# Linear attention and a multiplicative feed-forward on one core: batch 0's third and fourth query chunks, the order of two weight loads, and the last batch's layout

## The chip, the cores and the metric

The kernel runs on 1 core of one Trainium2 chip. The metric is the device time in microseconds of one execution; a kernel's time is the median of its runs. The profiled execution is one run with the hardware profiler on; its span is the time from its first to its last instruction in the profile.

## The reference

Eight batches, eight heads, 576 positions, 64 dimensions. The features of q and k are `relu(x)` times a cosine and a sine of the position, side by side, so 128 features per head. The attention is linear (no softmax). Its output, laid out as 4608 tokens by 512, goes through a feed-forward that is linear behind a product of two projections:

```python
kv  = einsum('bhsf,bhsd->bhfd', phi(k), v)
z   = phi(k).sum(axis=2)
num = einsum('bhsf,bhfd->bhsd', phi(q), kv)
den = einsum('bhsf,bhf->bhs', phi(q), z)[..., None] + 1e-06
x   = (num / den).transpose(0, 2, 1, 3).reshape(4608, 512)
out = ((x @ w1) * (x @ w2)) @ w3 @ w_out      # 512->1024, 1024->1024, 1024->512
```

## The kernel before

**Attention, by batch.** A batch's 576 positions are five chunks: four of 128 rows and one of 64 (the "half chunk", chunk 4). `features` makes cosine features on VectorE (L270) and sine features on ScalarE (L274), in bf16. `kv_first` (batch 0) and `kv_chunk` (L305) multiply k's features with v and a column of ones, so that the denominators come along. For a query chunk, the features must be transposed (features on the partitions): by TensorE into a bank of the accumulator memory and an eviction (`q_tr`, L336), or by a DMA transpose issued on SP's queue (`transpose_q`, L283). `num` (L365) multiplies them with the kv state, and VectorE normalizes (L381 to L383: denominator, reciprocal, product) into a block `xblk`. `x_tr` transposes that block again, by TensorE and an eviction (L417, L419) or by a DMA, into `xT`, the feed-forward's input.

**Feed-forward, by tiles.** Nine tiles of 512 tokens. `ffn_groups(t)` is a generator that makes one group of products per step: `products` (L462, w1 and w2), ScalarE copies one side out, VectorE multiplies with the other (L468, L519) into `abT`, and products with `w34b` (L532) give the output, which ScalarE evicts (L539) into `osb`. `w34b = w3 @ w_out` is computed once, in tile 0: for each of eight 128-row blocks of w3, `w3_tr` (L225) transposes the block on TensorE and VectorE copies it, and `w34_mm` (L237) multiplies it with w_out, in two parts of four products (part 0 reads w_out's first half, part 1 its second).

**The order is written by hand.** Between feed-forward groups, numbered slots run the functions entered by `at(slot, ...)`. Every engine executes its own instructions in that program order and waits on semaphores for data and for buffers. Tile 0's first four column blocks are made in two halves of 256 tokens, the first as quarters of 128, so that the first group can start when the first chunk (128 tokens) of `xT` is there, and the second quarter when the second chunk is there (slot 1 makes it).

**The start.** Lines 589 to 620 run ahead of slot 0. `idle_mms` are products of zeros whose result is not read. For chunk 0 the transposes are evicted by VectorE in halves; chunks 1, 2 and 3 are evicted by ScalarE (`q_tr(..., evac=False)[1]()`). The transposes of `q_tr`, `x_tr` and `w3_tr` share two buffers of one bank each (`ps_tr`). Chunk 3's transposes stand in slot 1, its cosines and sines at L606 and L607. The idle products' bank, `unread`, and the bank beside it belong to the pool `ps_idle`, which is closed when the feed-forward's four banks are opened.

**Queues.** All casting loads are issued on GpSimd's queue, in program order: v, q in two halves of columns, w1 and w2 in blocks of 256 columns, the half chunk of q (L201), then a block of w1. `other_loads` (L204) waits by a small copy for the first `xblk`, and issues the rest of w1 and w2, then `w3` block 0, w_out half 0, `w3` block 1, w_out half 1, `w3` blocks 2, 3, 4 and 5, batch 1's k, and `w3` blocks 6 and 7. An issue also waits until the load eight places before it has landed. SP's queue holds k's loads of batch 0, the DMA transposes and, at the end, the stores of the last tile; other stores are GpSimd's.

**Layouts.** Batches 1 to 6 are loaded in two parts: positions 0 to 319 into partitions 0 to 63 (five per partition), and 320 to 575 into partitions 64 to 127 (four per partition). Batch 0, and before the change also batch 7, are loaded as rows 0 to 511 over 128 partitions (four per partition) and rows 512 to 575 (the half chunk). `rows_of` gives the matching pieces of the output: one piece of 128 rows for batches 0 and 7, two of 64 for the others. The last tile of all (t = 8) holds chunks 0 to 3 of batch 7; its last 128 tokens are made, evicted (L550) and stored in two halves of 256 columns.

Of the kernel before, what the change touches and what calls it, by code (L numbers as in the profile page):

```python
# [68 lines left out]
def kernel(  # L69
# [41 lines left out]
    def load(b, which, part=None):  # L111
        for name in which:
            src = {"k": k, "v": v, "q": q}[name]
            if b == B - 1:
                if part == 0:
                    raw[b, name] = ld.tile([P, H, NCH, D], BF16, name=name + "s",
                                           bufs=2 if name == "q" else 1)
                (load_first4 if part else load_first)(nc.gpsimd, raw[b, name], src, b=b)
                continue
            if part != 1:  # L120
                raw[b, name] = ld.tile([P, H, NCH, D], BF16, name=name + "s",
                                       bufs=2 if name == "q" else 1)
                nc.gpsimd.dma_start(
                    out=raw[b, name][0:64, :, :, :].rearrange("p h j d -> p h (j d)"),
                    in_=src[b, :, 0:320, :].rearrange("h (p j) d -> p h (j d)", j=5))
            if part != 0:
                nc.gpsimd.dma_start(
                    out=raw[b, name][64:128, :, 0:4, :].rearrange("p h j d -> p h (j d)"),
                    in_=src[b, :, 320:S, :].rearrange("h (p j) d -> p h (j d)", j=4))

    def load_first(eng, t, src, c0=0, n=4, b=0):
        rows = src[b, :, 0:512, :].rearrange("h (p j) d -> p h j d", j=4)
        eng.dma_start(out=t[:, :, c0:c0 + n, :].rearrange("p h j d -> p h (j d)"),  # L133
                      in_=rows[:, :, c0:c0 + n, :].rearrange("p h j d -> p h (j d)"))

    def load_first4(eng, t, src, b=0):
        eng.dma_start(out=t[0:64, :, 4, :], in_=src[b, :, 512:S, :].rearrange("h p d -> p h d"))

    woutb = wst.tile([P, 8, DM], BF16, name="woutb")
    w3b = wst.tile([P, 8, DFF], BF16, name="w3b")  # L140
# [6 lines left out]
    def load_w3(jp, n):  # L147
        nc.gpsimd.dma_start(out=w3b[:, jp:jp + n, :],
                            in_=moe_w3[ds(jp * P, n * P), :].rearrange("(b p) l -> p b l", p=P))

    def load_wout(half):
        nc.gpsimd.dma_start(out=woutb[:, ts(half, 4), :],
                            in_=moe_w_out[ts(half, 512), :].rearrange("(c p) m -> p c m", p=P))
# [29 lines left out]
    def idle_mms(n):  # L183

        for _ in range(n):
            nc.tensor.matmul(unread[:, :], lhsT=zeros[:, 0:128], rhs=zeros[:], start=True, stop=True)
# [11 lines left out]

    load_w12(0, 256)
    load_w12(256, 256)  # L200
    load_first4(nc.gpsimd, q0, q)  # L201
    nc.gpsimd.dma_start(out=w1b[:, :, ds(512, 256)], in_=w1v[:, :, ds(512, 256)])

    def other_loads(behind):  # L204

        seen = sm.tile([P, 1], BF16, name="seen", bufs=1)
        nc.gpsimd.tensor_copy(out=seen[:], in_=behind)
        nc.gpsimd.dma_start(out=w2b[:, :, ds(512, 256)], in_=w2v[:, :, ds(512, 256)])
        load_w12(768, 256)
        for jp in range(2):  # L210
            load_w3(jp, 1)
            load_wout(jp)
        for jp in range(2, 4):
            load_w3(jp, 1)
        load_w3(4, 2)
        load(1, "k")
        load_w3(6, 2)
# [47 lines left out]
    def features(b, dst, src, c, cos=True, sin=True, scalar_heads=H):  # L265

        R = ROWS[c]
        at = c if b in (0, B - 1) else NCH + c
        if cos:
            nc.vector.tensor_scalar(out=dst[:R, c, :, 0:D], in0=src[:R, :, c, :], scalar1=0.0,  # L270
                                    scalar2=cosv[:R, at:at + 1], op0=ALU.max, op1=ALU.mult)
        if sin:
            n = scalar_heads
            nc.scalar.activation(out=dst[:R, c, 0:n, D:F], in_=src[:R, 0:n, c, :], func=ACTF.Relu,  # L274
                                 scale=sinv[:R, at:at + 1], bias=0.0)
            if n < H:
                nc.vector.tensor_scalar(out=dst[:R, c, n:H, D:F], in0=src[:R, n:H, c, :],
                                        scalar1=0.0, scalar2=sinv[:R, at:at + 1],
                                        op0=ALU.max, op1=ALU.mult)
# [51 lines left out]
    def q_tr(b, c, evac=True):  # L331
        R = ROWS[c]
        qp = feat[b][1]
        pst = ps_tr.tile([P, 8, 128], BF16, name="pst")
        for h in range(H):
            nc.tensor.transpose(pst[:, h, :], qp[:, c, h, :], identb[:])  # L336
        dst, src = att_of(b)["qpT"][:, :, ds(columns_of(b, c), R)], pst[:, :, 0:R]
        on_vector = lambda: nc.vector.tensor_copy(out=dst, in_=src)
        on_scalar = lambda: nc.scalar.copy(out=dst, in_=src)
        if evac:  # L340
            on_vector()
        return on_vector, on_scalar
# [55 lines left out]

    xT = {}

    def x_tr(b, c, by_vector=False):
        R, rows = ROWS[c], out_rows(b, c)
        xblk = att[b]["x"].pop(c)
        xf = xblk[:].rearrange("p g h d -> p (g h d)")
        if b % 2 == 0:
            slot = S * b + 128 * c
        else:
            slot = S * b + (0 if c == 4 else 64 + 128 * c)
        t, o = divmod(slot, 512)
        if t not in xT:  # L410
            xT[t] = xtp.tile([P, 4, 512], BF16, name="xT")
        if b >= 2 or (b, c) in ((0, 4), (1, 3)):
            nc.sync.dma_start_transpose(out=xT[t][:, :, ds(o, R)], in_=xf[rows])
            return
        pst = ps_tr.tile([P, 8, 128], BF16, name="pst")
        for kc in range(4):
            nc.tensor.transpose(pst[:, kc, :], xf[:, ts(kc, 128)], identb[:])  # L417
        copy = nc.vector.tensor_copy if by_vector else nc.scalar.copy
        copy(out=xT[t][:, :, ds(o, R)], in_=pst[:, 0:4, rows])  # L419

    def rows_of(b, c, n):

        if b in (0, B - 1):
            rows = out[ds(b * S, S), :]
            if c == 4:
                return [rows[512:S, :].rearrange("(p j) m -> p j m", j=1)]
            return [rows[0:512, :].rearrange("(p j) m -> p j m", j=4)[:, c:c + n, :]]
        lower = out[ds(b * S, 320), :].rearrange("(p j) m -> p j m", j=5)
        upper = out[ds(b * S + 320, 256), :].rearrange("(p j) m -> p j m", j=4)
        return [h[:, c:c + n, :] for h in ((lower,) if c == 4 else (lower, upper))]  # L430

    def store(eng, osb, g, n, cols=slice(0, DM)):

        pair, r = divmod(g, 9)
        b, c = (2 * pair, r) if r < 4 else (2 * pair + 1, r - 5)
        if r == 4:
            parts = rows_of(2 * pair, 4, 1) + rows_of(2 * pair + 1, 4, 1)
        elif n == 1 or c + n <= 4:
            parts = rows_of(b, c, n)
        else:  # L440
            parts = None
        if parts is None or (r == 4 and n > 1):
            for i in range(n):
                store(eng, osb[:, i:i + 1, :], g + i, 1, cols)
            return
        for i, rows in enumerate(parts):
            eng.dma_start(out=rows[:, :, cols], in_=osb[64 * i:64 * i + rows.shape[0], :, cols])  # L447

    ffn_tiles = [0]

# [5 lines left out]
    def ffn_groups(t):  # L456
# [86 lines left out]
        if t == NT - 1:  # L543
            for half in range(2):
                cols = ts(half, 256)
                ops = ffn_tile()
                for jc in range(8):
                    nc.tensor.matmul(ops[:, 0:256], lhsT=abT[:, jc, ts(3, 128)],  # L548
                                     rhs=w34b[:, jc, cols], start=(jc == 0), stop=(jc == 7))
                nc.scalar.copy(out=osb[:, 1, cols], in_=ops[:, 0:256])  # L550
                store(nc.sync, osb[:, 1:2, :], 4 * t + 3, 1, cols)
                yield


# [47 lines left out]
    idle_mms(1)  # L602
    num(0, 0)
    q_tr(0, 1, evac=False)[1]()
    other_loads(att[0]["x"][0][:, 0, 0, 0:1])
    features(0, q0f, q0, 3, sin=False)  # L606
    features(0, q0f, q0, 3, cos=False)  # L607
    idle_mms(2)
    x_tr(0, 0, by_vector=True)
    num(0, 1)  # L610
    q_tr(0, 2, evac=False)[1]()
    ps_ffn = []
    for stack in first:
        stack.close()
# [2 lines left out]
                                                     space=bass.MemoryType.PSUM)))  # L617


    at(1, lambda: x_tr(0, 1, by_vector=True), lambda: q_tr(0, 3, evac=False)[1](), lambda: num(0, 2))  # L620
    at(3, lambda: x_tr(0, 2), lambda: num(0, 3))
    at(5, lambda: x_tr(0, 3))
    at(6, lambda: features(0, q0f, q0, 4))
    at(23, lambda: transpose_q(0, 4))
    at(7, lambda: load(1, "qv"), lambda: load(2, "q"))
    at(29, lambda: num(0, 4))
# [70 lines left out]
```

## Time and profile before

| what | value |
|---|---|
| time, median of 3 runs | 248.81 us (248.33 to 248.97) |
| profiled execution, own time | 248.81 us |
| its span | 246.9 us |
| TensorE products (PE), busy | 240.5 us, 97% |
| VectorE (DVE), busy | 135.9 us, 55% |
| ScalarE (ACT), busy | 130.2 us, 53% |
| GpSimd (POOL), busy | 93.4 us, 38% |
| granted TensorE clock | 1.0 |

How to read it: an engine that is busy 97% of the span sets the time, so what counts is where it is idle or does work that nobody needs, and which event ends each of these stretches. Engines at about half of the span matter only where TensorE waits for them. In the timelines a row gives start and duration in microseconds, the engine, the source line, the operation, what it writes and reads, its shape and count; a bracket gives the idle time before it and what ended it. The landing time of a load is its issue time plus its time to landing.

The longest waits of TensorE in the whole execution:

```profile
PE unread L186 <- DVE zeros L162: 1.2, 1, 1.2
PE kva L322 <- DVE va L297: 1.2, 1, 1.2
PE pst L349 <- DVE qp L277: 0.3, 1, 0.3
```

(waiting line, what it waited for, total us, times, longest.) The first two lie ahead of batch 0's kv products, at the very start.

### The profile page before, as it was taken

The page shows a single profiled execution, that of the slowest core. Times are in us where ns is not written, and L with a number is a line of the kernel's source. Part 1 is how long each engine was busy: PE and PEld are TensorE (multiplying, and loading weights), DVE is VectorE, ACT ScalarE, POOL GpSimd, SP SyncE. Part 2 cuts the span into 40 slices and gives each one's busy share as a digit, 9 for nine tenths or more (in the row PEclk, how much of TensorE's full clock was granted, in tenths as well). Part 3 has the DMA queues.
Part 4 walks back from the last instruction along what each step waited for, and adds up shares of the span by engine and source line. Part 5 has one row for each costly group of instructions (what it writes and reads, how often), then busy time and mean ns, then how long its engine had stood idle before and what let it go on. Part 6 is the DMA issues. An engine that isn't in the chain of part 4 may idle for free.

```text
span 246.9 us, 5034 instructions
## 1 busy us (share of the span) xinstructions
PE 240.5 (97%) x1872; PEld 130.4 (53%) x1872; DVE 135.9 (55%) x336; ACT 130.2 (53%) x266; POOL 93.4 (38%) x196
## 2 busy tenths in 40 slices
PE   8799999999999999999999999999999999999994
PEld 3479545566975445444544555454545554444443
DVE  7775652668968445647566475547464645312420
ACT  2676313767943873466556654854575333434332
POOL 7654342024512261127032612173322005978700
PEclk9999999999999999999999999999999999999999
DMA  7999999999999969999999999999994536998823
GB/s 199 178 194 199 201 207 204 198 181 173 153 162 142 167 100 149 132 149 134 169 144 155 118 180 150 150 140 140 166 142 89 94 64 214 260 281 289 282 101 128
DMA packets 86200, 41.22 MB, mean 167 GB/s; under 512 B 53792, under 2 KB 82720, under 8 KB 86176
## 3 DMA queue, kind: packets, MB, share of 16 engines
q0 software_dynamic: 37008, 27.20, 71.8%
q1 hardware_dynamic: 49168, 13.71, 35.9%
q8 instruction: 14, 0.23, 0.4%
q14 instruction: 10, 0.08, 0.1%
HBM read 38.80 MB, written 9.44 MB: 195 GB/s over the span
## 4 chain that ended last, share of the span: by engine, by line
PE 85%; DMA 10%; POOL 3%; issue 1%; ACT 0%; POOLq 0%
PE ffnps L462 45%; PE ffnps L532 24%; PE ffnps L237 6%; DMA woutb<-in_moe_w_out_dram 5%; DMA w2b<-in_moe_w_dram 5%; PE pnum L365 4%; PE pnum L305 4%; PE pst L225 1%; PE ffnps L548 1%; POOL qs L133 1%; POOL w1b L196 1%; PE pst L336 1%; POOL vs L133 0%; PE pst L417 0%; POOL w2b L197 0%
## 5 line engine op out<-in xcount | busy, mean ns | idle before, releaser
L462 PE MATMUL ffnps<-xT,w2b 128*128 128x512 bf16 (+2 forms) x344 | 75.5, 344 | 0.0
L462 PE MATMUL ffnps<-xT,w1b 128*128 128x512 bf16 (+2 forms) x344 | 75.5, 344 | 0.0
L519 DVE TENSOR_TENSOR abT<-asb,ffnps 128x512 bf16<-128x512 bf16 x64 | 43.9, 686 | 54.3 <-PE ffnps L462 52.4
L532 PE MATMUL ffnps<-w34b,abT 128*128 128x512 bf16 x280 | 65.0, 379 | 0.0
L515 ACT CAST asb<-ffnps 128x512 bf16<-128x512 f32 x64 | 37.4, 584 | 50.0 <-PE ffnps L462 45.2
L462 PEld LDWEIGHTS <-w2b 128*128 128x128 bf16 x344 | 31.0, 98 | 27.3
L462 PEld LDWEIGHTS <-w1b 128*128 128x128 bf16 x344 | 30.8, 98 | 25.9
L567 POOL COPY seen<-mark 1x1 bf16<-1x1 bf16 x50 | 8.9, 178 | 84.4 <-ACT mark L565 84.4
L532 PEld LDWEIGHTS <-abT 128*128 128x128 bf16 x280 | 26.0, 98 | 27.9 <-DVE abT L519 0.2
L539 ACT COPY osb<-ffnps 128x512 f32<-128x512 f32 x35 | 20.5, 584 | 35.2 <-PE ffnps L532 35.1
L274 ACT ACTIVATE qp<-qs,sinv 128x512 bf16<-128x512 bf16 (+2 forms) x40 | 28.1, 714 | 1.8 <-DMA qs<-in_q_dram 1.8
L383 DVE TENSOR_TENSOR xblk<-pnum,den 128x512 bf16<-128x512 f32 (+1 forms) x37 | 25.6, 691 | 1.3
L297 POOL COPY va<-vs 128x512 bf16<-128x512 bf16 (+1 forms) x30 | 17.6, 621 | 22.9 <-DMA vs<-in_v_dram 22.4
L274 ACT ACTIVATE kp<-ks,sinv 128x512 bf16<-128x512 bf16 (+1 forms) x35 | 25.0, 717 | 0.9 <-DMA ks<-in_k_dram 0.9
L447 POOL DMA_DIRECT2D out_dram<-osb x42 | 22.1, 531 | 2.7 <-issue 2.1
L365 PEld LDWEIGHTS <-qpT 128*128 128x128 bf16 x320 | 15.4, 98 | 8.7 <-DVE qpT L350 0.6
L381 DVE TENSOR_SCALAR den<-pnum 128x8 f32<-128x8 f32 (+1 forms) x37 | 6.0, 163 | 22.6 <-PE pnum L365 22.5
L237 PE MATMUL ffnps<-woutb,w3T 128*128 128x512 bf16 x64 | 15.8, 380 | 0.2 <-DMA woutb<-in_moe_w_out_dram 0.2
L365 PE MATMUL pnum<-kvs,qpT 128*128 128x65 bf16 x296 | 15.8, 194 | 0.0
L270 DVE TENSOR_SCALAR qp<-qs,cosv 128x512 bf16<-128x512 bf16 (+1 forms) x40 | 15.3, 389 | 0.7 <-DMA qs<-in_q_dram 0.7
L305 PEld LDWEIGHTS <-kp 128*128 128x128 bf16 x280 | 11.4, 98 | 4.1
L270 DVE TENSOR_SCALAR kp<-ks,cosv 128x512 bf16<-128x512 bf16 (+1 forms) x35 | 12.5, 367 | 0.0
(88 smaller groups left out, 181.6 us busy)
## 6 DMA issues: line engine op xcount, KB each, us to landing
out_dram<-osb POOLq DMA_DIRECT2D x16, 256.0 KB, 4.5
out_dram<-osb POOLq DMA_DIRECT2D x24, 128.0 KB, 3.9
qs<-in_q_dram POOLq DMA_DIRECT2D x8, 256.0 KB, 7.6
ks<-in_k_dram POOLq DMA_DIRECT2D x6, 320.0 KB, 6.3
qs<-in_q_dram POOLq DMA_DIRECT2D x6, 320.0 KB, 5.9
vs<-in_v_dram POOLq DMA_DIRECT2D x6, 320.0 KB, 5.7
ks<-in_k_dram POOLq DMA_DIRECT2D x6, 256.0 KB, 7.0
vs<-in_v_dram POOLq DMA_DIRECT2D x6, 256.0 KB, 5.4
```

The source lines that it names most:

```text
L237: nc.tensor.matmul(acc[:, :], lhsT=w3T[:, lc, :], rhs=woutb[:, lc, :], start=(lc == 0), stop=(lc == 7))
L270: nc.vector.tensor_scalar(out=dst[:R, c, :, 0:D], in0=src[:R, :, c, :], scalar1=0.0, scalar2=cosv[:R, at:at + 1], op0=ALU.max, op1=ALU.mult)
L274: nc.scalar.activation(out=dst[:R, c, 0:n, D:F], in_=src[:R, 0:n, c, :], func=ACTF.Relu, scale=sinv[:R, at:at + 1], bias=0.0)
L305: nc.tensor.matmul(kvt[:, h // 4, ds((h % 4) * 65, 65)], lhsT=kp[:, c, h, :], rhs=va[:, c, h, 0:D + 1], start=(i == 0 and h % 4 == 0), sto ...
L365: nc.tensor.matmul(banks[h // 4][:, ds((h % 4) * 65, 65)], lhsT=qpT[:, h, ds(at, 128)], rhs=kvs[:, h, :], start=True, stop=True)
L383: nc.vector.tensor_tensor(out=xblk[rows, g], in0=n4[:, :, :, 0:D], in1=den[rows, g].unsqueeze(3).to_broadcast([R, G, 4, D]), op=ALU.mult)
L447: eng.dma_start(out=rows[:, :, cols], in_=osb[64 * i:64 * i + rows.shape[0], :, cols])
L462: nc.tensor.matmul(out, lhsT=w[:, kc, ts(jc, 128)], rhs=x[:, kc, tok], start=(kc == 0), stop=(kc == 3))
L515: nc.scalar.copy(out=asb[:], in_=aT[:, :])
L519: nc.vector.tensor_mul(out=abT[:, jc, :], in0=asb[:], in1=bT[:, :])
L532: nc.tensor.matmul(ops[:, :], lhsT=abT[:, jc, ts(ms, 128)], rhs=w34b[:, jc, :], start=(jc == 0), stop=(jc == 7))
L539: nc.scalar.copy(out=osb[:, ms % 2, :], in_=ops[:, :])
```

## The change

Four things are changed.

- **The order at the start.** Chunk 2's transposes are issued ahead of the transposes of the first `xblk`, and two idle products there are dropped. The first block is transposed into a new tile of the idle products' bank and evicted by ScalarE instead of VectorE; chunk 2's eviction follows it on ScalarE. Chunk 3's transposes move from slot 1 to the place where chunk 2's stood.
- **The sines of chunk 3** are made by one GpSimd instruction instead of one of ScalarE. It stands on GpSimd's queue ahead of `other_loads`.
- **Loads.** The half chunk of q is loaded behind `w3` block 1 instead of ahead of the third w1 block, and its features move from slot 6 to slot 19. Both halves of w_out are loaded ahead of `w3` block 1.
- **The last batch** is loaded and stored in the layout of batches 1 to 6. So each store of 128 rows in the last tile becomes two of 64; the two of the very last stores' pieces are issued on SP and on ScalarE.

```diff
@@ load
-            if b == B - 1:
-                if part == 0:
-                    raw[b, name] = ld.tile([P, H, NCH, D], BF16, name=name + "s",
-                                           bufs=2 if name == "q" else 1)
-                (load_first4 if part else load_first)(nc.gpsimd, raw[b, name], src, b=b)
-                continue
@@ loads of the start
     load_w12(256, 256)
-    load_first4(nc.gpsimd, q0, q)
     nc.gpsimd.dma_start(out=w1b[:, :, ds(512, 256)], in_=w1v[:, :, ds(512, 256)])
@@ other_loads
-        for jp in range(2):
-            load_w3(jp, 1)
-            load_wout(jp)
+        load_w3(0, 1)
+        for half in range(2):
+            load_wout(half)
+        load_w3(1, 1)
+        load_first4(nc.gpsimd, q0, q)
@@ features
-        at = c if b in (0, B - 1) else NCH + c
+        at = c if b == 0 else NCH + c
@@ x_tr
-        pst = ps_tr.tile([P, 8, 128], BF16, name="pst")
+        if pst is None:
+            pst = ps_tr.tile([P, 8, 128], BF16, name="pst")
@@ rows_of
-        if b in (0, B - 1):
+        if b == 0:
@@ store
-            eng.dma_start(out=rows[:, :, cols], in_=osb[64 * i:64 * i + rows.shape[0], :, cols])
+            on = eng[i % 2] if isinstance(eng, tuple) else eng
+            on.dma_start(out=rows[:, :, cols], in_=osb[64 * i:64 * i + rows.shape[0], :, cols])
@@ ffn_groups, last tokens
-                store(nc.sync, osb[:, 1:2, :], 4 * t + 3, 1, cols)
+                store((nc.sync, nc.scalar), osb[:, 1:2, :], 4 * t + 3, 1, cols)
@@ the start
     q_tr(0, 1, evac=False)[1]()
+    nc.gpsimd.tensor_scalar(out=q0f[:, 3, :, D:F], in0=q0[:, :, 3, :], scalar1=0.0,
+                            scalar2=sinv[:, 3:4], op0=ALU.max, op1=ALU.mult)
     other_loads(att[0]["x"][0][:, 0, 0, 0:1])
     features(0, q0f, q0, 3, sin=False)
-    features(0, q0f, q0, 3, cos=False)
-    idle_mms(2)
-    x_tr(0, 0, by_vector=True)
+    by_scalar = q_tr(0, 2, evac=False)[1]
+    x_tr(0, 0, pst=ps_idle.tile([P, 8, 128], BF16, name="unread"))
+    by_scalar()
     num(0, 1)
-    q_tr(0, 2, evac=False)[1]()
+    q_tr(0, 3, evac=False)[1]()
@@ slots
-    at(1, lambda: x_tr(0, 1, by_vector=True), lambda: q_tr(0, 3, evac=False)[1](), lambda: num(0, 2))
+    at(1, lambda: x_tr(0, 1, by_vector=True), lambda: num(0, 2))
-    at(6, lambda: features(0, q0f, q0, 4))
+    at(19, lambda: features(0, q0f, q0, 4))
```

## The prediction

> **What bounds the kernel now.** I read the chain that ended last first, then TensorE's timeline, then the waits of the other engines beside it, then the landings of single loads.
>
> ```profile
> PE 85%; DMA 10%; POOL 3%; issue 1%; ACT 0%; POOLq 0%
> ```
>
> This is the chain's split by engine. TensorE holds 85%, and the loads' 10% is two pieces (8.13 to 19.62 and 20.43 to 33.98 us). TensorE works 240.5 of 246.9 us, so only the few places where it is not yet, or no longer, back to back can move the end. Its timeline shows them:
>
> ```profile
> 13.62 0.61 PE L336 MATMUL pst<-identb,qp 128*128 128x128 bf16 x8
> 14.07 0.59 PE L186 MATMUL unread<-zeros 128*128 128x512 bf16 x2
> 15.01 0.40 PE L417 MATMUL pst<-identb,xblk 128*128 128x128 bf16 x4 [0.34 <-DVE xblk L383]
> 15.34 0.43 PE L365 MATMUL pnum<-kvs,qpT 128*128 128x65 bf16 x8
> 15.61 0.61 PE L336 MATMUL pst<-identb,qp 128*128 128x128 bf16 x8
> 16.05 0.39 PE L462 MATMUL ffnps<-xT,w1b 128*128 128x128 bf16 x4
> ...
> 16.99 0.40 PE L417 MATMUL pst<-identb,xblk 128*128 128x128 bf16 x4
> 17.32 0.61 PE L336 MATMUL pst<-identb,qp 128*128 128x128 bf16 x8
> 17.76 0.42 PE L365 MATMUL pnum<-kvs,qpT 128*128 128x65 bf16 x8
> 18.02 0.39 PE L462 MATMUL ffnps<-xT,w1b 128*128 128x128 bf16 x4
> ...
> 33.23 0.61 PE L225 MATMUL pst<-identb,w3b 128*128 128x128 bf16 x8
> 34.02 1.89 PE L237 MATMUL ffnps<-woutb,w3T 128*128 128x512 bf16 x8 [0.18 <-DMA woutb<-in_moe_w_out_dram]
> ```
>
> Start and duration are the first two columns; the bracket is idle time and what ended it. From 14.07 to 15.01 TensorE has two filler products and a wait for the first xblk. After 15.34 its one named idle time up to the last product (ending 243.72) is the 0.18 us for w_out's second half. So the change can gain in the head, at 34 us, and in the tail of 246.9 - 243.72 = 3.2 us.
>
> **The head: eight transposes moved into the wait.** Eight transposes take 14.07 - 13.62 = 0.45 us of TensorE's order. Chunk 2's go from 15.61 to 14.07, in place of the two fillers; they need the features of chunk 2 (ACT ends 12.61 + 1.34 = 13.95; DVE 13.34 + 0.34 = 13.68) and fit, ending at 14.52, before xblk. Chunk 3's go from 17.32 to 15.61. At most 0.45 us of TensorE order is saved in front of 18.02. What the rest allows:
>
> - First products, 16.05. The copy of the first transposed block goes from VectorE (15.44 to 15.86) to ScalarE, behind the eviction of 14.27 to 15.28. The same copy on ScalarE took 0.58 us (the row of 20.21), so it ends near 15.44 + 0.58 = 16.02. TensorE is free at 16.05: cost 0. Its own bank spares the two transpose buffers, which chunks 2 and 3 now hold.
> - Next on ScalarE is chunk 2's eviction, 1.01 us, overlapping by 0.1 as neighbours there do: 15.92 to 16.93. It frees the buffer of the transposes at 16.99, which anyhow wait for xblk (VectorE, 16.24 + 0.69 = 16.93). Cost 0.
> - Second quarter, 18.02. It needs VectorE's copy:
>
> ```profile
> 17.42 0.42 DVE L419 COPY xT<-pst 128x512 bf16<-128x512 bf16 x1 [0.49 <-PE pst L417]
> ```
>
> It ends at 17.84 and starts no earlier than now, since it follows the block at 16.99. Without chunk 3's transposes TensorE is ready at about 17.47, but must wait until some 17.86. So of the 0.45 only 18.02 - 17.86 = 0.16 us is gained: a new wait on this copy takes the place of the removed work.
>
> **The sines on GpSimd.** The old instruction was ScalarE's at 15.18 (0.72 us). The new one waits for the second query load, issued at 5.03 and landed 8.0 us later, 13.03; GpSimd reacted 0.25 us after other landings (19.62 to 19.90), so it starts near 13.3. Before shows no such operation there. From below: its 128x512 copies, 0.62 us. From above: two such, one per arithmetic step, 1.24 us. Either ends by 14.6, while chunk 3's transposes want it at 15.61; the next on GpSimd's queue waits for xblk (15.01) anyway. The cover is 1.0 us. I take the copy's end, since it too reads one operand.
>
> VectorE can suffer beside it. These are its feature rows while GpSimd copied from 62.72 to 65.66:
>
> ```profile
> 63.65 0.37 DVE L270 TENSOR_SCALAR qp<-qs,cosv 128x512 bf16<-128x512 bf16 x1
> 63.94 0.69 DVE L270 TENSOR_SCALAR kp<-ks,cosv 128x512 bf16<-128x512 bf16 x1
> 64.56 0.67 DVE L468 TENSOR_TENSOR abT<-asb,ffnps 128x512 bf16<-128x512 bf16 x1
> 65.16 0.65 DVE L270 TENSOR_SCALAR qp<-qs,cosv 128x512 bf16<-128x512 bf16 x1
> ```
>
> L270 takes 0.34 us elsewhere, so two of three lost up to 0.35; L468, which reads an accumulator, lost nothing. At 13.34 VectorE runs L270 for chunk 2, just where the sines start, and the chain den, reciprocal, xblk (13.82 to 14.95) is behind it with a slack of 13.82 - 13.68 = 0.14. A loss of 0.35 would put xblk and the first products 0.21 later, and the second quarter at 17.15 + 0.43 + 0.42 + 0.03 = 18.03: the 0.16 is gone. So the head brings between 0.0 and 0.16. I take 0.05, nearer the loss, because the overlap is almost full.
>
> The Trainium skill bears on this pair. "SBUF — State Buffer" (on the shared port pair) says that VectorE in a two-port mode and GpSimd hold the pair by turns, and the loser is blocked for the whole instruction. By that rule L270 is blocked for all of the sines if these start first, 0.6 us or more, and the head loses some 0.3 us; by the rows above it loses 0.0 to 0.35 and the head is no worse than even. No row here separates the two.
>
> **The loads.** GpSimd's queue moves w_out's second half ahead of the second w3 block, and the half query chunk (64 KB) from 10.03 to behind both. That half chunk's features and DMA transposes move too, from the sixth slot to the nineteenth (after 37 us). The loads run as one full stream, 190 to 210 GB/s from 8 to 50 us, so each lands when the bytes ahead of it are done. Landings now, issue plus time: w3 block 1 at 31.2, w_out half 2 at 33.95. In the new order w3 block 1 is last of the pair. Only the 64 KB fewer ahead: 33.95 - 64 KB at 190 KB per us (0.34) = 33.6. The chunk's transposes, issued at 23.68, also leave that stretch:
>
> ```profile
> q0 software_dynamic: 779, 0.95, 100.2%
> q1 hardware_dynamic: 544, 0.13, 20.3%
> ```
>
> (window 27 to 32.5 us: packets, MB, share.) The loads moved 0.95 MB in 5.5 us, 173 GB/s, against 1.13 MB in the next 5.5 us, 206: 0.18 MB, 0.9 us of stream, goes to those 544 packets. Without them w3 block 1 lands near 33.6 - 0.9 = 32.7, w_out half 2 one 256 KB block (1.3 us) earlier. TensorE asks for the w3 block at 33.23 less the head's gain, at least 33.07, so no wait. The 0.18 goes, but the following product pair then waits for its transposed w3 as all later ones do (36.19 to 38.02 is 1.83, 34.02 to 35.75 only 1.73): 0.10 back, net gain 0.08. If it lands at 33.6 instead, its transposes (0.44) start at 33.64 and products at 34.09: loss 0.07. I take 0.08.
>
> Late next: the last two w3 blocks land at 30.51 + 14.1 = 44.6, with the same bytes in front by then, and are asked for at 44.83. So the head's gain is capped at some 0.2 us. And the half chunk: features after product 37.05, ScalarE's eviction to 37.84, sines 0.72 more, DMA transposes issued near 38.4, and, at the 9.2 us that the same transfer took in the full stream, landed at 47.6, for products at 48.41 less the gain. Cover 0.6 us or more; hidden.
>
> **The last batch and the tail.** Its loads become 320 and 256 KB instead of 512 and 64. Its V landed at 183.9 and the GpSimd copies ended at 186.8, for products at 187.46; the other batches' V parts took 5.5 and 5.4 us, which gives 181.8 and 183.7: no worse, 0. Its stores split by partition halves: on SP two issues of 0.33 us per 1.72 us, hidden. The last tile's halves go to SP and ScalarE. Last eviction 243.76 to 244.13, issue 244.17, landed 1.8 us later, end 246.9. Same bytes, so 0 there. But ScalarE issues the first half's store between its two last evictions, from 243.26 to the need at 243.76: free below 0.46 us. SP's store rows say 0.33; its longest plain issue 0.73, its longest issue of any kind but a queue stall 1.29. Bounds: gain 0.1 (fewer rows per issue), loss 0.73 - 0.46 = 0.27, far end 0.83; I take 0.
>
> "DMA: Bandwidth & Descriptors" (rules for kernel authors) speaks against the split: transfers to two partition halves share the same engines, use one transfer. By the rule the tail gains nothing; no row here shows both forms.
>
> **The sum**: 0.05 + 0.08 + 0 = 0.13 us. The profiled run took 248.81 with a span of 246.9 (1.9 around it), which is also the median. 248.81 - 0.13 gives 248.68, rounded 248.7. Below 0.3% (0.75 us) a measurement of this kernel, whose three runs spread 0.64, can't tell a change.
>
> **The rivals.**
>
> 1. *All of it comes through* (0.16): full 0.16, the 0.18 without give-back, tail 0.1, and the runs' scatter of 0.3: 248.81 - 0.74 = 248.0. For it: every piece has a row. Against: the caps at 17.86 and 44.6.
> 2. *ScalarE's issue blocks the last eviction* (0.11): decides from 0.46 us on; at 1.29, 0.83 is lost: 248.81 + 0.83 - 0.13 = 249.5, slower. For it: no store was issued there before. Against: SP's 0.33.
> 3. *The half chunk's transposes come late* (0.08): over 0.6 us beyond 47.6; at 2 us beyond, 1.4 lost: 250.1, slower. For it: the stream is as full there, and 9.2 is one sample. Against: those 544 packets alternated one to one with load packets, which are smaller after 42 us.
> 4. *The reorder doesn't do what it says*: w3 block 1 waits in place of w_out, with contention in the head: 248.81 + 0.07 = 248.9, within 0.3%.
>
> **How the numbers follow.** Within 0.3%: my forecast 0.50 and rival 4 with 0.15, 0.65 together. Faster: rival 1, 0.16. Slower: rivals 2 and 3, 0.19. The likeliest case alone spans 248.3 to 249.0; the range goes to rival 1's end and to the 0.27 of the tail with the scatter: 248.0 to 249.4.
>
> **What would show it.** Right: TensorE at 14.07 on transposes; products still near 16.05 to 16.25; a wait of 0.1 to 0.4 us before the second quarter, named for VectorE's copy; none for w_out; the last product 0.1 to 0.2 us earlier. Wrong: sines over 2.3 us, a wait at 33 us named for w3, idle time before the batch's last products at 48, or a last eviction beginning over 0.1 us after its products.

## The result and the profile after

| | before | after |
|---|---|---|
| median of six runs each | 248.78 us (248.33 to 249.55) | 250.13 us (249.87 to 250.95) |
| ratio, 95% interval | | 1.0059 [1.0037, 1.0081] |
| profiled execution, own time | 248.81 us | 250.29 us |
| its span | 246.9 us | 248.4 us |
| TensorE products, busy | 240.5 us | 240.4 us |

The kernel is slower, by some 1.4 us, and the interval lies wholly above 1. TensorE does the same work at the same clock (granted 1.00 up to 247 us in both profiles; the 0.998 of after, taken over its whole span, comes from the last 1.4 us, in which no product runs), so the 1.5 us of span is idle time. The chain that ended last, by engine, after:

```profile
PE 90%; DMA 3%; DVE 3%; issue 1%; POOL 1%; ACT 0%; ACTq 0%; POOLq 0%; DVEq 0%
```

The loads' 10% of before has become 3%. That alone tells nothing of the time: a chain's shares change when another of two near-equal paths is followed back. TensorE's timeline of after, the rows that answer to those of before:

```profile
15.50 0.40 PE L413 MATMUL unread<-identb,xblk 128*128 128x128 bf16 x4 [0.34 <-DVE xblk L378]
15.73 0.42 PE L360 MATMUL pnum<-kvs,qpT 128*128 128x65 bf16 x8
15.99 0.61 PE L331 MATMUL pst<-identb,qp 128*128 128x128 bf16 x8
16.57 0.38 PE L458 MATMUL ffnps<-xT,w1b 128*128 128x128 bf16 x4
...
18.38 0.38 PE L458 MATMUL ffnps<-xT,w1b 128*128 128x128 bf16 x4 [0.26 <-DVE xT L415]
...
33.13 1.04 PE L232 MATMUL ffnps<-woutb,w3T 128*128 128x512 bf16 x4 [0.31 <-DVE w3T L222]
34.00 0.61 PE L220 MATMUL pst<-identb,w3b 128*128 128x128 bf16 x8
34.45 1.77 PE L232 MATMUL ffnps<-woutb,w3T 128*128 128x512 bf16 x7
...
36.72 0.81 PE L232 MATMUL ffnps<-woutb,w3T 128*128 128x512 bf16 x3
```

The reader is to see three things. The second quarter (18.38) now waits 0.26 us for VectorE's copy, as forecast. The wait for w_out is gone. And ahead of the first w3 products, where nothing waited, TensorE now waits 0.31 us for VectorE's copy of the first transposed w3 block. The rows of before that answer to 33.13 and 36.72:

```profile
32.36 1.04 PE L237 MATMUL ffnps<-woutb,w3T 128*128 128x512 bf16 x4
...
36.19 1.34 PE L237 MATMUL ffnps<-woutb,w3T 128*128 128x512 bf16 x5
```

The end of the kernel, ScalarE's timeline in before and then in after (the first pair are the last two evictions; L443 are the new store issues):

```profile
242.89 0.37 ACT L550 COPY osb<-ffnps 128x256 f32<-128x256 f32 x1 [0.29 <-PE ffnps L548]
243.76 0.37 ACT L550 COPY osb<-ffnps 128x256 f32<-128x256 f32 x1 [0.50 <-PE ffnps L548]
```

```profile
243.42 0.37 ACT L546 COPY osb<-ffnps 128x256 f32<-128x256 f32 x1 [0.29 <-PE ffnps L544]
243.82 0.56 ACTq L443 DMA_DIRECT2D out_dram<-osb  x1
244.42 0.37 ACT L546 COPY osb<-ffnps 128x256 f32<-128x256 f32 x1 [0.63 <-PE ffnps L544]
244.82 0.48 ACTq L443 DMA_DIRECT2D out_dram<-osb  x1
```

The issue took 0.56 us where 0.46 were free, and the last eviction's idle time grew from 0.50 to 0.63. From the start of that eviction to the end of the span it was 246.9 - 243.76 = 3.14 us before, and 248.4 - 244.42 = 3.98 us after.

So the two profiles can be cut at five events. Each row is the time from the event above it:

| event | before | after | difference |
|---|---|---|---|
| first kv product | 10.11 | 10.44 | +0.33 |
| second quarter's products | 7.91 | 7.94 | +0.03 |
| products behind the third w3 transposes | 18.17 | 18.34 | +0.17 |
| last eviction's start | 207.57 | 207.70 | +0.13 |
| end of the span | 3.14 | 3.98 | +0.84 |

(Starts: 18.02 and 18.38; 36.19 and 36.72; 243.76 and 244.42.) They add up to the 1.50. Over half lies behind the last product, where the prediction counted 0.

### The profile page after: what moved, and what is told of

Its sections match the earlier page's. It is cut to its first block, busy times and chain, and to the rows that moved or that the text cites. A ratio compares the mean times of both kernels' runs of the same rounds, so it can differ in the third digit from the quotient of the medians.

```text
span 248.4 us, 5042 instructions
## 1 busy us (share of the span) xinstructions
PE 240.4 (97%) x1870; PEld 130.3 (52%) x1870; DVE 136.7 (55%) x335; ACT 130.1 (52%) x266; POOL 94.8 (38%) x197
## 4 chain that ended last, share of the span: by engine, by line
PE 90%; DMA 3%; DVE 3%; issue 1%; POOL 1%; ACT 0%; ACTq 0%; POOLq 0%; DVEq 0%
PE ffnps L458 49%; PE ffnps L528 24%; PE ffnps L232 6%; PE pnum L360 4%; PE pnum L300 4%; DMA qs<-in_q_dram 3%; PE pst L220 1%; PE pst L331 1%; PE pst L413 1%; DVE abT L515 1%; POOL vs L127 0%; DVE qp L265 0%; PE ffnps L544 0%; DVE qpT L345 0%; ACT osb L546 0%
## 5 line engine op out<-in xcount | busy, mean ns | idle before, releaser
L269 ACT ACTIVATE qp<-qs,sinv 128x512 bf16<-128x512 bf16 (+2 forms) x39 | 27.4, 715 | 2.1 <-DMA qs<-in_q_dram 2.1
L443 POOL DMA_DIRECT2D out_dram<-osb x42 | 22.1, 531 | 2.7 <-issue 2.3
L265 DVE TENSOR_SCALAR qp<-qs,cosv 128x512 bf16<-128x512 bf16 (+1 forms) x40 | 16.7, 426 | 0.6 <-DMA qs<-in_q_dram 0.6
```

The source lines that it names most:

```text
L443: on.dma_start(out=rows[:, :, cols], in_=osb[64 * i:64 * i + rows.shape[0], :, cols])
```

## The experiments

The runs of before beside them had medians of 248.79 us (29 runs, beside the first four kernels) and 248.94 us (34 runs, beside the last four). The theory to test: the 64-row stores cost most, a late VectorE instruction ahead of the w3 copies costs the rest, and the new head gives nothing. The rivals: ScalarE's queue as such, the slow sines, and the scatter of the first kv product.

### Each half of the change alone

`e1_head_only` is after with the last batch's layout and stores of before; `e2_tail_only` is before with those of after.

```diff
 e1 (against after), shortened; e2 (against before) is the reverse of it
+            if b == B - 1:
...
+                (load_first4 if part else load_first)(nc.gpsimd, raw[b, name], src, b=b)
+                continue
...
-        at = c if b == 0 else NCH + c
+        at = c if b in (0, B - 1) else NCH + c
...
-        if b == 0:
+        if b in (0, B - 1):
...
-                store((nc.sync, nc.scalar), osb[:, 1:2, :], 4 * t + 3, 1, cols)
+                store(nc.sync, osb[:, 1:2, :], 4 * t + 3, 1, cols)
```

> The changed kernel with the last batch's layout and the last stores of the kernel before, so only the start and the load order are changed. Theory (two thirds of the loss are 64-row stores in the tail): time 0.0 to 0.4 us over before (ratio 1.000 to 1.0015), last eviction to end of the span 2.7 to 2.8 us as in before. Rival (the start loses it, by the sines on GpSimd and the w3 copies): 1.0 us or more over before, ratio 1.004 or more. In both, the sines take some 2.0 us and VectorE's cosines beside them 0.7 to 0.8.

> The kernel before with only the last batch's layout and the last stores of the changed kernel. Theory: 0.8 to 1.1 us over before (ratio 1.003 to 1.0045), and from the last eviction's start to the end of the span 3.9 to 4.1 us against 3.14. Rival (the start loses it): within 0.3 us of before.

Measured: e1 249.47 us (248.87 to 251.07, 12 runs), ratio 1.0018 [0.9995, 1.0040]. e2 250.00 us (249.22 to 250.71, 12 runs), ratio 1.0030 [1.0009, 1.0051]. In e1 the last stretch is 247.8 - 244.65 = 3.15 us, as in before; in e2 it is 248.2 - 244.24 = 3.96, as in after, and ScalarE's issue (0.55 us) again pushed the last eviction (idle 0.62). The layout and its stores alone make the kernel slower by some 0.75 us (0.0030 of 248.8; the medians differ by 1.21), and of the two halves this is the one whose interval excludes 1. The head's 0.45 us (1.0018; by the medians 0.68) can't be told from nothing by its runs, but its trace has the same 0.31 us wait as after:

```profile
32.81 1.04 PE L238 MATMUL ffnps<-woutb,w3T 128*128 128x512 bf16 x4 [0.31 <-DVE w3T L228]
```

### The 64-row stores without ScalarE's queue, and that queue without them

`e3_tail_sp` is after with both halves of the very last stores on SP. `e4_halves_only` is before with each store of the last tile as two DMAs of 64 partitions, all on SP, and nothing else. `e7_whole_scalar` is before with the last two stores whole but issued on ScalarE.

```diff
 e3 (against after)
-store((nc.sync, nc.scalar), osb[:, 1:2, :], 4 * t + 3, 1, cols)
+store(nc.sync, osb[:, 1:2, :], 4 * t + 3, 1, cols)
 e4 (against before), in store
+if eng is nc.sync:
+    for lo in (0, 64):
+        eng.dma_start(out=rows[lo:lo + 64, :, cols], in_=osb[lo:lo + 64, :, cols])
+    continue
 e7 (against before)
-store(nc.sync, osb[:, 1:2, :], 4 * t + 3, 1, cols)
+store(nc.scalar, osb[:, 1:2, :], 4 * t + 3, 1, cols)
```

> The changed kernel, but both pieces of the last two stores are issued on SP, none on ScalarE. Theory (the 64-row transfers themselves are slow, 165 ns for a 2 KB packet against 87): the last eviction starts 0.1 to 0.15 us earlier relative to the last product, but SP now issues two of 0.5 us behind it, so the time stays within 0.4 us of the changed kernel, 249.9 to 250.5. Rival (a store issued on ScalarE is what costs): the time falls by 0.8 us or more, to 249.3 or below.

> The kernel before, layout and loads unchanged, but each store of the last tile is issued as two transfers of 64 partitions, both on SP. Theory: packets of 2 KB take about 165 ns in place of 87, the last stores land 0.6 us or more later, time 0.7 to 1.3 us over before. Rival (the layout of the last batch, its loads or the order of rows in memory, is what costs): within 0.3 us of before.

> The kernel before with its last two stores, whole ones of 128 rows, issued on ScalarE in place of SP. Theory (64-row transfers are slow, not ScalarE's queue): an issue takes 0.33 to 0.36 us, the last eviction starts as long after the last products as before (idle 0.50), from its start to the end of the span 3.0 to 3.2 us; time within 0.3 us of before. Rival (stores issued on ScalarE cost): last eviction 0.13 us or more later, 3.5 us or more to the end.

Measured: e3 251.43 us (251.10 to 251.73, 7 runs), ratio 1.0089 [1.0060, 1.0118]. e4 250.96 us (250.41 to 252.25, 7 runs), ratio 1.0076 [1.0046, 1.0107]. e7 248.79 us (248.21 to 250.66, 10 runs), ratio 1.0010 [0.9985, 1.0035]. The last stretch is 249.5 - 244.21 = 5.29 us in e3, 249.5 - 244.26 = 5.24 in e4, and 247.0 - 243.83 = 3.17 in e7. So ScalarE's queue costs nothing where a whole store is issued on it, and it makes the split stores cheaper, not dearer. The split costs, and e4 shows it with the layout and the loads of before. e3 and e4 came out dearer than their own forecasts (at most 250.5 us, and at most 1.3 us over before): that four halved issues in a row would make SP's queue late was not counted.

What the DMA queues moved from 238 to 250 us (GB/s in 40 slices of 0.3 us; then queue, packets, MB, and the time of its packets as a share of 16 engines over the 12 us), in before, after and e4 in turn:

```profile
GB/s 0 0 0 0 0 0 68 396 375 34 0 0 198 389 287 0 0 0 287 396 338 287 3 215 222 0 0 0 0 0 0 0 0 0 0 0 0 0 0 0
q1 hardware_dynamic: 720, 1.05, 24.3%
```

```profile
GB/s 0 0 0 0 0 0 0 0 0 75 225 191 219 157 7 191 212 205 191 75 34 198 191 219 198 147 232 304 174 51 0 0 0 0 0 0 0 0 0 0
q1 hardware_dynamic: 640, 0.92, 34.1%
q10 hardware_dynamic: 160, 0.13, 4.6%
```

```profile
GB/s 0 0 0 0 0 0 0 0 0 109 198 205 212 150 0 198 205 219 212 41 48 205 178 225 198 181 58 147 72 113 106 89 130 0 0 0 0 0 0 55
q1 hardware_dynamic: 800, 1.05, 40.8%
```

The same 1.05 MB occupied the engines for 38.7% in after against 24.3%: 1.6 times as long. A store of 128 rows runs at 390 GB/s, a store of 64 rows at 180 to 225; only where two queues have one each in flight (232 and 304, after) is it more. The issues are dearer too. Their rows in before, after, e4 and e7 (start, duration of all, count):

```profile
239.17 5.32 SPq L447 DMA_DIRECT2D out_dram<-osb  x5
```

```profile
239.70 5.84 SPq L443 DMA_DIRECT2D out_dram<-osb  x8
```

```profile
239.67 7.13 SPq L449 DMA_DIRECT2D out_dram<-osb  x10
```

```profile
243.36 0.37 ACTq L447 DMA_DIRECT2D out_dram<-osb  x1
```

The last of before's five ends at 244.5, but the last of e4's ten at 246.8, though its last eviction is over at 244.63: SP's queue became late. In after the last issue on SP ends at 239.70 + 5.84 = 245.54, which is 1.12 us after the last eviction's start, against 244.49 - 243.76 = 0.73 in before. So 0.39 of the 0.84 us is spent up to the end of SP's issues, and the other 0.45 behind them, while the last transfers finish. One issue took 0.33 us on SP before, 0.47 to 0.59 (median 0.55) for 64 rows after; on ScalarE 0.37 and 0.34 whole, 0.56 and 0.48 halved. ScalarE's issue of a whole store fits in the 0.46 us and the last eviction's idle time stays 0.50:

```profile
243.83 0.37 ACT L550 COPY osb<-ffnps 128x256 f32<-128x256 f32 x1 [0.50 <-PE ffnps L548]
```

### The late VectorE instruction

In the record of VectorE (semaphore records counted too), one instruction of the first 100 starts 0.4 us later than its waits allow: the one at place 63, counted from 0, whatever it is. VectorE's timeline, the two first 512-wide products of the feed-forward, in before, after, and `e5_two_memsets` and `e6_sines_vector` described below:

```profile
27.34 0.69 DVE L519 TENSOR_TENSOR abT<-asb,ffnps 128x512 bf16<-128x512 bf16 x1 [1.12 <-PE ffnps L462]
28.66 0.69 DVE L519 TENSOR_TENSOR abT<-asb,ffnps 128x512 bf16<-128x512 bf16 x1 [0.63 <-PE ffnps L462]
```

```profile
27.30 0.69 DVE L515 TENSOR_TENSOR abT<-asb,ffnps 128x512 bf16<-128x512 bf16 x1 [0.71 <-PE ffnps L458]
29.43 0.69 DVE L515 TENSOR_TENSOR abT<-asb,ffnps 128x512 bf16<-128x512 bf16 x1 [1.45 <-PE ffnps L458]
...
32.39 0.68 DVE L222 COPY w3T<-pst 128x1024 bf16<-128x1024 bf16 x1
```

```profile
27.08 0.69 DVE L524 TENSOR_TENSOR abT<-asb,ffnps 128x512 bf16<-128x512 bf16 x1 [1.12 <-PE ffnps L467]
28.40 0.69 DVE L524 TENSOR_TENSOR abT<-asb,ffnps 128x512 bf16<-128x512 bf16 x1 [0.63 <-PE ffnps L467]
```

```profile
26.66 0.69 DVE L521 TENSOR_TENSOR abT<-asb,ffnps 128x512 bf16<-128x512 bf16 x1 [0.72 <-PE ffnps L464]
28.38 0.69 DVE L521 TENSOR_TENSOR abT<-asb,ffnps 128x512 bf16<-128x512 bf16 x1 [1.04 <-PE ffnps L464]
```

Read e6 as both on time: idle 0.72 and 1.04. In before (and e5) the first is 0.40 us late, and the second, on time, follows sooner. In after the second is late, 1.45 against 1.04. TensorE doesn't need the first at once, but behind the second stand batch 1's memsets (1.5 us), one more product and the first w3 copy, with no such time to spare. Up to there the change takes two records out of VectorE's stream, so place 63 falls on the second product instead of the first.

`e5_two_memsets` tests just that: e1 with two memsets of one column put at the start of VectorE's stream. `e6_sines_vector` tests the slow sines, and shifts the stream too: e1 with chunk 3's sines on VectorE, behind its cosines. `e8_combined` is e6 with batch 1's memsets five slots earlier.

```diff
 e5 (against e1)
+    spare = const.tile([P, 2], FP32, name="spare")
+    for i in range(2):
+        nc.vector.memset(spare[:, i:i + 1], 0.0)
 e6 (against e1)
-    nc.gpsimd.tensor_scalar(out=q0f[:, 3, :, D:F], in0=q0[:, :, 3, :], ...)
     features(0, q0f, q0, 3, sin=False)
+    nc.vector.tensor_scalar(out=q0f[:, 3, :, D:F], in0=q0[:, :, 3, :], ...)
 e8 (against e6)
-    at(11, lambda: feature_buffers(1))
+    at(6, lambda: feature_buffers(1))
```

In the expectations "third w3 transposes" stands for the products behind them, the row of 36.72 above.

> The first experiment's kernel (only the start and the load order changed) with two tiny memsets more on VectorE at the very start, where it waits for the k load. They write a tile that nobody reads; they only move every later VectorE instruction two places on. Theory (VectorE's instruction at place 63 of its stream starts about 0.45 us late whatever it is, and the change moved that place from the first to the second 512-wide product with w2, in front of the memsets and the first w3 copy): the late one is the first product again, TensorE's wait for the first w3 copy falls from 0.31 us to 0.1 or less, and from the first kv product to the third w3 transposes it is 25.7 to 25.95 us in place of 26.2 to 26.3. Time 0.2 to 0.5 us below the first experiment. Rival (the sines' contention or the load order makes that wait): 0.31 us of wait and 26.2 or more stay.

> The first experiment's kernel with chunk 3's sines on VectorE, behind its cosines, in place of GpSimd. Theory: chunk 2's cosines take 0.34 us again in place of 0.76, the first block's transposes come 0.15 to 0.2 us earlier after the first kv product (4.85 in place of 5.0), the second quarter 0.1 to 0.2 us earlier (7.7 to 7.8 in place of 7.9). One more VectorE instruction puts place 63 on a semaphore wait that is early anyway, so the wait for the first w3 copy falls as well. Rival (the sines cost nothing, since the second quarter was 7.9 with and without them): the second quarter stays at 7.9.

> The kernel before with the changed start and load order, sines of chunk 3 on VectorE, and the memsets of batch 1's buffers in slot 6 in place of 11. Theory: no wait for the first w3 copy, none for w_out, second quarter at 7.7 to 7.8 us after the first kv product; third w3 transposes at 25.4 to 25.6; tail as before. Time 0.1 to 0.5 us below before (ratio 0.998 to 0.9995), perhaps not to be told from 1. Rival (the changed order at the start loses in itself): ratio above 1.001.

Measured, 12 runs each: e5 248.85 us (248.02 to 249.73), ratio 1.0002 [0.9983, 1.0021]. e6 248.54 us (247.97 to 250.41), ratio 0.9992 [0.9971, 1.0013]. e8 248.96 us (248.25 to 250.44), ratio 1.0006 [0.9984, 1.0028]. The stretches of every kernel's profile (us):

| kernel | first kv product to second quarter | from there to the products behind the third w3 transposes | TensorE's wait there |
|---|---|---|---|
| before | 7.91 | 18.17 | w_out 0.18 |
| e2 / e4 / e7 (head of before) | 7.85 / 7.77 / 7.92 | 17.93 / 17.93 / 17.93 | none |
| after, e1, e3 (head of after) | 7.94 / 7.89 / 7.90 | 18.34 / 18.33 / 18.34 | first w3 copy 0.31 |
| e5 (two memsets more) | 7.80 | 17.93 | none |
| e6 (sines on VectorE) | 7.73 | 17.92 | none |
| e8 (and memsets earlier) | 7.66 | 17.85 | none |

The middle column splits cleanly: 17.93 where nothing waits, 18.34 with the late second product, so that costs 0.41 us. Two memsets of no use, which only shift the stream, take the 0.41 away with everything else of the head in place: that mechanism is shown. It is the traces that show it; by the runs alone e5 and e1 can't be told apart (1.0002 and 1.0018, with intervals that overlap). And the wait for w_out, which one part of the change was to remove, appears in one of four profiles with before's head. It cost 0.24 us there (18.17 - 17.93); in e2, e4 and e7 nothing is lost there with the old order of loads. (e4 has a wait of 0.2 us for a w3 block, but at 44.97 us, behind this stretch.) The new order alone was not tried.

The sines are the row that is furthest from its forecast. GpSimd's sines and VectorE's cosines of chunk 2 beside them, in after, then the same cosines in e6:

```profile
13.58 1.99 POOL L601 TENSOR_SCALAR qp<-qs,sinv 128x512 bf16<-128x512 bf16 x1 [2.48 <-DVE qpT L345]
```

```profile
13.64 0.76 DVE L265 TENSOR_SCALAR qp<-qs,cosv 128x512 bf16<-128x512 bf16 x1
```

```profile
13.18 0.34 DVE L271 TENSOR_SCALAR qp<-qs,cosv 128x512 bf16<-128x512 bf16 x1
```

The sines took 1.99 us instead of 0.62 to 1.24, and the cosines lost 0.42. Yet the second quarter came only some 0.15 us earlier without them (7.73 against 7.88, the mean of after, e1, e3 and e5).

e8 got what it was to get by 36 us, and its profiled execution, at 249.84 us well above its own median, lost more than that later, to 0.6 us waiting for a VectorE product and 0.4 us of which the profile names no cause. Such stalls of 0.2 to 0.6 us come in some executions of several kernels (e1 and e2 among them), and are why a profile's span alone can't rank these kernels. e8's forecast, 0.1 to 0.5 us below before, did not come true by its runs (1.0006), though the interval reaches down to 0.9984. No kernel here is faster than before by more than its interval; e5, e6 and e8 have after's order at the start without its late product and without the split stores, and their intervals lie wholly below after's.

## Why the prediction was wrong

The forecast was no change, at 248.7 us within 248.0 to 249.4; it is 250.13, slower by 0.59%. By its steps:

- **"Same bytes, so 0 there", of the last stores: the step that failed.** Bytes were the wrong measure. The stores of 64 rows move half as fast and take 0.55 us to issue instead of 0.33, and the tail is 0.84 us longer in after, 0.82 in e2. The working had looked at SP's queue ("two issues of 0.33 us per 1.72 us, hidden") but took the issue time of a whole store for the half; the bounds of the tail, 0.1 gain to 0.27 loss (far end 0.83), were for ScalarE's issue alone, so the price had no place in them at all. The 0.1 gain supposed that fewer rows are issued faster; the runs show the opposite.
- **ScalarE's issue ahead of the last eviction, taken at 0.** The mechanism and the limit of 0.46 us were right: 0.56 us was needed and 0.13 us lost. Rival 2 named it, with 0.83, worked out from 1.29, the size of another kind of issue (of which one, at 67.44 in before, took 1.37). The halved store is what makes it: a whole one, in e7, cost 0.
- **Loads, net gain 0.08.** w_out's wait went, no w3 block was late, the products at 48 us had no wait, so rivals 3 and 4 didn't occur; that rival 3's figure, 250.1, is close to the measured time is chance. But the 0.18 was one execution's, not the kernel's, and the late VectorE instruction took 0.41 in its place. The prediction followed VectorE's chain only as far as the copy at 17.42. That an edit moves later instructions along an engine's stream was not costed, and nothing in before's profile priced it, though the 1.12 of before's first product beside the 0.63 of its second is that row.
- **Sines, 0.62 to 1.24 us.** They took 1.99, outside both bounds: two copies were not a bound from above. The named cover held all the same: they ended at 15.57, and chunk 3's transposes ran at 15.99.
- **The head, 0.05.** Right within 0.1: the first quarter came 0.19 us later (16.57 - 10.44 against 16.05 - 10.11), the second was held by VectorE's copy for 0.26 us, and came at 7.94 against 7.91 (7.88 and 7.86 as means of four), so nothing was gained. VectorE's loss beside GpSimd was 0.42, near the 0.35 read off its rows, and the later wait absorbed most of it. Of the rule that the loser is blocked for the whole instruction, the run shows 0.42 us lost beside an operation of 1.99; whether the cosines ran in the mode that the rule is about, no run shows.
- **The first kv product**, 10.44 against 10.11, is scatter: e1 and e3, with the same head as after, have 10.18 and 10.24, and kernels with before's have 9.98 to 10.23.
- **Rival 1's sum** is 0.07 off: 248.81 - 0.74 is 248.07, not 248.0. Nothing hangs on it.

The Trainium skill had the rule for the failing step. "SBUF — State Buffer", section "Door 1: The DMA port swizzle", says that the partitions from 0 to 63, and those from 64 to 127, reach only half of the 16 ports, and so half of the DMA bandwidth. The rates agree, 180 to 225 GB/s against 390; which ports a transfer used, no run here shows. The prediction weighed the rule of "DMA: Bandwidth & Descriptors" against splitting into halves, and read from it that the split gains nothing; the runs show that it loses, 0.84 us on two queues and 2.1 us (5.24 - 3.14, e4) on one.

## What to carry to other kernels

A store at the very end has nothing behind it, so its layout is part of the critical path: keep the last tile's stores on all 128 partitions, and price a split by the half's own rate and issue time, not by its bytes. Before counting a wait of 0.2 us as a gain, see it in more than one execution. And when an edit adds or takes instructions on an engine, look at which later ones change places as well as at the edited lines.

## What the runs showed of the hardware

- VectorE's instruction at place 63 of its record starts 0.45 us behind the end of the wait ahead of it, in before, after, e1 to e5 and e7, where the same operation at other places starts 0.04 behind; those at places 191 and 447 start 0.40 to 0.42 us behind theirs in six of the ten kernels, and ScalarE's at place 63 starts 0.34 to 0.37 behind in nine of the ten. All these places are one less than a multiple of 64, but VectorE's at 127, 255, 319 and 383 are not seen late in any profile. No other instruction of the two engines is seen over 0.2 us late in this way. What makes it is not recorded, and no run here tells it.
- An issue of a 64-row store took 0.47 to 0.60 us, one of 128 rows 0.33 to 0.37, though it moves twice the bytes.
- GpSimd took 1.99 us (in after, e1, e3 and e5 alike) for a multiplication by a value per partition on 128x512 in bf16 (with the maximum ahead of it), beside 0.34 us for the like operation on VectorE and 0.62 us for a GpSimd copy of that shape.
